# Extra 60-column products ahead of some TensorE steps, in a kernel with a planned order

## The chip, the cores and the metric

The kernel runs on one core of one Trainium2 chip. The metric is the device time of one execution in microseconds (us). A core has several engines that run side by side: TensorE (PE in the profile) multiplies matrices, ScalarE (ACT) and VectorE (DVE) compute elementwise and reduce, GpSimd (POOL) only sets up constants here, and SyncE (SP) issues DMA transfers. TensorE writes its products into PSUM, a memory of eight banks of 512 fp32 columns on 128 partitions; ScalarE and VectorE read them there.

## The reference

```python
scores = scale * np.matmul(q, k.transpose(0, 1, 3, 2))      # q, k, v: 4 x 8 x 576 x 64
scores = np.where(masks, scores, -1e9)                      # a window of 32; heads 4..7 dilated by 4
attn = softmax(scores)
x = np.matmul(attn, v)                                      # -> 2304 tokens x 512
h = x @ w_in                                                # 512 -> 1024
solu = h * softmax(h)
x = layernorm(solu) * g_ln @ w_out                          # 1024 -> 512
h = x @ w_in2                                               # 512 -> 2048
return softplus(h) @ w_out2                                 # 2048 -> 512
```

All inputs and the output are fp32. The kernel splits most operands into two fp16 halves, high and low, and adds three fp16 products (high-high, high-low, low-high).

## The kernel before, in words

The attention is cut into 28 pairs of blocks. A block takes 80 or 96 query rows of four heads. Its products are called QK (scores), PV (probabilities times values), and, for the first ten pairs, t, tp and tx (transposes by TensorE). The first ten pairs work in fp32; the others work in fp16 halves and transpose by DMA. Eighteen token tiles of 128 go through the first layer (m1a and m1b: 12 products of 512 columns each) and the normalisation. Nine groups of 256 tokens go through w_out (ya, yb: 24 products of 256 columns), the hidden layer (h: 24 products of 256 columns) and the output (o: 12 products of 512 columns). The weights are read as fp32, scaled and split; for the scale a small product sums squares over the partitions (w1im, w2o2m and the like, and pre0m to pre3m for q, k and v).

The order is written by a planner (class Plan, line 105). Every step is an operation with a cost per engine (`pe_cost`, line 203, for TensorE), the operations that it follows, and the buffers that it uses. A table of due times (DUE, line 254) gives priorities. The planner walks through time, starts on each engine the most urgent operation that is ready, and notes the start as `t0` (line 176). At the end (lines 1283 to 1285) each operation's function is called in that order. `pin` keeps each engine's instructions in the order in which they were called; the framework adds the semaphores by which one engine waits for another. So the planner fixes only each queue's order; at run time an instruction starts when its engine is free and its semaphores allow.

Four PSUM tiles, bank0 to bank3, of one bank each are shared among the small products:

```python
banks = [psum.tile([128, 512], FP32, name=f"bank{i}") for i in range(4)]      # line 398
ps_x.add(banks[1], place=taken[1])                                            # 402
for x in (1, 0, 2, 3):
    ps_v.add(banks[x], place=taken[x])                                        # 408
```

Bank 1 holds the output of PV in columns 0 to 259 and the transposed result of tx in columns 260 to 451 (`px` and `xt`, lines 871 and 872), and the sums for the scales in its first columns. VectorE or ScalarE reads PV's part to normalise it (into xf), and both read tx's part to cast it into xr, the input of the first layer. Columns 452 to 511 are written by nothing. `mm` (line 432) is one product. `eye`, a 128 x 128 identity in bf16, is made by GpSimd at the start, as is its fp32 twin `eye32`, which the first transposes need.

Of the kernel before, what the change touches and what calls it, by code (L numbers as in the profile page):

```python
# [216 lines left out]
def kernel(  # L217
# [12 lines left out]
    nc = tc.nc  # L230
# [57 lines left out]
    def mem(shape, dt, name):  # L288
        return const.tile(shape, dt, name=name)
# [3 lines left out]
    eye = mem([128, 128], BF16, "eye")  # L293
# [104 lines left out]
    banks = [psum.tile([128, 512], FP32, name=f"bank{i}") for i in range(4)]  # L398
# [13 lines left out]
    pin = tc.keep_in_program_order  # L412
# [19 lines left out]
    def mm(out, l, r, start, stop):  # L432
        pin(nc.tensor.matmul(out, l, r, start=start, stop=stop))  # L433
# [845 lines left out]
    for p in (qk_pool, qT_pool, kT_pool, pT_pool, xd_pool):  # L1279
        for s in p.slots:  # L1280
            if s[3] is not last_w and not s[3]:
                s[3].extend(last32)
    order = P.order()
    for o in order:
        o.fn(o.on)


# [28 lines left out]
```

## Time and profile before

| | |
|---|---|
| median of 3 runs | 772.14 us (771.76 to 773.48) |
| the profiled execution | 773.81 us, span 772.1 us |
| mean granted TensorE clock | 0.956 of full speed |
| busy: TensorE, VectorE, ScalarE | 92%, 75%, 62% |

The span runs from the first instruction to the last. A timeline row gives the start, the length of the run of like instructions, the engine, the source line (often that of a helper), the operation, output<-input, the shape and the count; in brackets stand the idle time of the engine before it and what ended that. [...] All views give times in us from the span's start.

### The profile page before, as it was taken

How to read it: one execution, taken by the hardware profiler on the slowest of the kernel's cores; microseconds unless marked ns; L12 is line 12 of the kernel's file. 1: busy time of each engine (PE TensorE's matmuls, PEld its weight loads, DVE VectorE, ACT ScalarE, POOL GpSimd, SP SyncE). 2: the span in 40 equal slices, each digit the busy share in tenths (PEclk: the TensorE clock that was granted, in tenths of full speed). 3: DMA queues.
4: the chain of work that ended last, by engine and by line, in shares of the span. 5: the costliest groups of instructions: out<-in, count | busy, mean ns of one | idle time of the engine just before them, and what ended most of it. 6: DMA issues, size and time to landing. Idle time of an engine off the chain costs nothing.

```text
span 772.1 us, 14234 instructions
## 1 busy us (share of the span) xinstructions
PE 708.1 (92%) x5176; PEld 495.2 (64%) x5176; DVE 579.9 (75%) x1646; ACT 478.0 (62%) x1057; POOL 3.5 (0%) x22
## 2 busy tenths in 40 slices
PE   6787989969968889999899999999999999999997
PEld 5574676745856447766756558676676568676673
DVE  1898978989999996696999997799955633534363
ACT  4575776757899856865787776656825524423351
POOL 1000000000000000000000000000000000000000
PEclk9999558968979999999999999999999999999999
DMA  8983773647895466824988788157403002100000
GB/s 223 253 259 132 207 178 104 175 104 164 157 183 138 93 160 176 220 60 107 176 163 145 149 145 160 36 110 123 83 11 82 1 1 56 28 1 28 1 28 28
DMA packets 187798, 89.80 MB, mean 116 GB/s; under 512 B 158032, under 2 KB 175440, under 8 KB 187728
## 3 DMA queue, kind: packets, MB, share of 16 engines
q1 hardware_dynamic: 187728, 88.90, 50.6%
q8 instruction: 40, 0.66, 0.4%
q14 instruction: 30, 0.25, 0.1%
HBM read 54.53 MB, written 4.72 MB: 77 GB/s over the span
## 4 chain that ended last, share of the span: by engine, by line
PE 46%; DVE 28%; ACT 11%; DMA 9%; issue 5%; SPq 0%; DVEq 0%; ACTq 0%
PE bank L433 23%; PE ps_w L433 21%; ACT a L415 4%; DVE s L941 3%; DVE W L424 3%; PE bank L436 2%; DMA pT<-p 2%; DVE E L424 2%; DVE r L424 2%; DVE p L427 2%; DMA E<-in_moe_w_out_dram 1%; DVE g L427 1%; DVE e L424 1%; ACT E L415 1%; ACT hl L415 1%
## 5 line engine op out<-in xcount | busy, mean ns | idle before, releaser
L433 PEld LDWEIGHTS <-W 128*128 128x128 f16 x2592 | 253.2, 98 | 46.3 <-issue 9.4
L433 PE MATMUL bank<-y,W 128*128 128x256 f16 x1728 | 199.0, 274 | 5.8 <-ACT r L415 2.4
L433 PE MATMUL ps_w<-W,g 128*128 128x512 f16 x864 | 194.8, 379 | 3.7 <-DVE s2i L419 1.3
L433 PEld LDWEIGHTS <-g 128*128 128x128 f16 x864 | 83.2, 98 | 97.0 <-DVE g L427 2.6
L433 PE MATMUL ps_w<-W,xr 128*128 128x512 f16 x432 | 106.0, 402 | 2.9 <-ACT osb L415 1.4
L415 ACT ACTIVATE a<-bank,invC 128x512 f32<-128x512 f32 x72 | 49.0, 681 | 85.1 <-PE bank L433 82.6
L433 PE MATMUL bank<-lnT,W 128*128 128x256 f16 x864 | 97.4, 273 | 2.2 <-DVE y L424 1.7
L415 ACT ACTIVATE a<-a 128x512 f32<-128x512 f32 x144 | 90.1, 627 | 2.5
L421 DVE TENSOR_SCALAR r<-bank,KR 128x512 f32<-128x512 f32 x44 | 33.0, 749 | 62.3 <-ACT a L415 57.7
L433 PEld LDWEIGHTS <-xr 128*128 128x128 f16 x432 | 43.7, 104 | 55.0 <-issue 14.0
L424 DVE SCALAR_TENSOR_TENSOR r<-a,KR,r 128x512 f32<-128x512 f32 x72 | 53.7, 746 | 14.8 <-ACT a L415 13.2
L415 ACT ACTIVATE s<-s 96x128 f32<-96x128 f32 (+3 forms) x144 | 43.6, 375 | 24.6 <-DVE s L421 18.7
L415 ACT ACTIVATE E<-E 128x768 f32<-128x768 f32 (+3 forms) x58 | 42.0, 725 | 18.0 <-DVE E L424 6.7
L427 DVE TENSOR_TENSOR g<-r,g 128x512 f16<-128x512 f32 x72 | 49.4, 687 | 3.2 <-DVE g L448 0.5
L941 DVE CUSTOM_DVE_ANT_0 s<-bank,band,bsc 96x128 f32<-96x128 f32 (+3 forms) x144 | 39.0, 324 | 1.5 <-PE bank L433 1.0
L433 PE MATMUL bank<-kT,qT 128*96 128x128 f16 (+7 forms) x288 | 31.2, 260 | 1.0 <-DMA kT<-qk 0.6
L415 ACT ACTIVATE y<-bank 128x512 f16<-128x512 f32 x16 | 9.5, 593 | 35.5 <-PE bank L433 35.5
L433 PEld LDWEIGHTS <-pT 128*96 128x96 f16 (+3 forms) x432 | 22.9, 125 | 13.1 <-DMA pT<-p 8.9
L433 PE MATMUL bank<-v,pT 128*96 128x65 f16 (+3 forms) x432 | 24.0, 207 | 7.5 <-DMA pT<-p 3.7
L415 ACT ACTIVATE e<-ps_w,st,bsc 128x1024 f32<-128x1024 f32 x16 | 19.2, 1200 | 18.3 <-DVE rs L419 9.5
L424 DVE SCALAR_TENSOR_TENSOR E<-E 128x512 int32<-128x512 int32 x44 | 28.6, 682 | 0.1
L1067 DVE TENSOR_REDUCE st<-ps_w 128x1 f32<-128x1024 f32 x18 | 21.8, 1218 | 8.8 <-PE ps_w L433 8.7
(196 smaller groups left out, 922.8 us busy)
## 6 DMA issues: line engine op xcount, KB each, us to landing
E<-in_moe_w_in_dram SPq DMA_DIRECT2D x18, 512.0 KB, 4.5
E<-in_moe_w_out_dram SPq DMA_DIRECT2D x18, 512.0 KB, 5.0
out_dram<-osb SPq DMA_DIRECT2D x18, 256.0 KB, 2.4
E<-in_q_dram SPq DMA_DIRECT2D x9, 384.0 KB, 3.3
E<-in_k_dram SPq DMA_DIRECT2D x9, 384.0 KB, 3.7
E<-in_v_dram SPq DMA_DIRECT2D x9, 384.0 KB, 3.5
W<-in_moe_w_in_dram SPq DMA_DIRECT2D x6, 512.0 KB, 6.5
W<-in_moe_w_out_dram SPq DMA_DIRECT2D x6, 512.0 KB, 5.2
```

What stands on the lines that cost most here:

```text
L415: pin(nc.scalar.activation(out=out, in_=in_, func=func, **kw))
L421: pin(nc.vector.tensor_scalar(out=out, in0=in0, scalar1=s1, scalar2=s2, op0=op0, op1=op1))
L424: pin(nc.vector.scalar_tensor_tensor(out=out, in0=in0, scalar=s, in1=in1, op0=op0, op1=op1, **kw))
L427: pin(nc.vector.tensor_tensor(out=out, in0=a, in1=b, op=op))
L433: pin(nc.tensor.matmul(out, l, r, start=start, stop=stop))
L436: pin(nc.tensor.transpose(out, in_, eye32[:in_.shape[0], :in_.shape[0]]))
L941: pin(nc.vector.tensor_tensor_reduce(out=sv()[:rows, h, :nk], in0=sb.t[:rows, h, :nk], in1=band[:rows, 48 - m:48 - m + nk], scale=sc[:rows ...
L1067: ({"DVE": (1.142, 0.14)}, lambda e: pin(nc.vector.tensor_reduce(out=col(0), in_=ph(), axis=AXX, op=ALU.max, negate=True)), [mb], [ps]),
```

## The change

Ahead of the loop that calls the operations, one product writes 60 columns that no other step uses. Then, for each TensorE operation that the planner starts before 300 us of its own time, the loop looks at the time between the end of the TensorE operation ahead of it and its start, both by the planner. It takes 0.3 us off, divides by 0.03 us, and issues that many products of the identity with its own first 60 columns into the same 60 columns of bank 1, just ahead of the operation. Nothing reads them. The planner, its costs and its order are as before.

```diff
     order = P.order()
+    spare = banks[1][:, 452:512]
+    mm(spare, eye, eye[:, 0:60], True, True)
+    free = 0.0
     for o in order:
+        if o.on == "PE":
+            if o.t0 < 300.0:
+                for _ in range(int((o.t0 - free - 0.3) / 0.03)):
+                    pin(nc.tensor.matmul(spare, eye, eye[:, 0:60], start=False, stop=False, skip_group_check=True))
+            free = o.t0 + o.opts["PE"][0]
         o.fn(o.on)
```

## Rows read from the trace of the kernel before

**Rows 1.** The page: busy time (share, instructions) of each engine; a DMA queue.
```profile
PE 708.1 (92%) x5176; PEld 495.2 (64%) x5176; DVE 579.9 (75%) x1646; ACT 478.0 (62%) x1057; POOL 3.5 (0%) x22
...
q8 instruction: 40, 0.66, 0.4%
```

**Rows 2.** By stretch: length, PE, PEld, DVE, ACT, POOL busy, granted clock, DMA, GB/s.
```profile
80.00:97.00 17.00, 17.00 (x69) 11.18 (x69) 16.23 (x45) 13.63 (x49) 0.00 (x0) 0.51 0.71 203
101.00:121.00 20.00, 19.16 (x100) 14.16 (x100) 16.66 (x54) 14.95 (x40) 0.00 (x0) 0.50 0.77 196
162.00:179.00 17.00, 13.29 (x64) 9.67 (x65) 15.02 (x70) 12.14 (x27) 0.00 (x0) 0.50 0.48 94
...
300.00:772.00 472.00, 454.56 (x3536) 316.05 (x3533) 323.38 (x906) 261.21 (x519) 0.00 (x0) 1.00 0.41 83
```

**Rows 3.** Timeline of TensorE: like work at either level.
```profile
52.30 2.02 PE L433 MATMUL bank<-qk,qT 64*96 64x128 f32 x8
...
153.25 1.11 PE L433 MATMUL bank<-kT,qT 64*96 64x128 f32 x8
...
116.71 4.93 PE L433 MATMUL ps_w<-W,xr 128*128 128x512 f16 x12
...
121.62 2.75 PE L433 MATMUL ps_w<-W,xr 128*128 128x512 f16 x12
```

**Rows 4.** Timeline of TensorE, the first 62 us.
```profile
4.20 0.79 PE L436 MATMUL bank<-eye,rk 80*128 80x80 f32 x4 [4.20 <-POOL eye L487]
...
7.25 1.48 PE L436 MATMUL bank<-eye,W 80*128 80x80 f32 x8 [1.72 <-DMA W<-in_k_dram]
...
23.43 1.25 PE L433 MATMUL bank<-xd,pT 80*80 80x65 f32 x8
...
28.36 0.58 PE L433 MATMUL bank<-band,eye 96*96 96x512 bf16 x1 [0.89 <-ACT qk L415]
...
32.53 1.33 PE L433 MATMUL bank<-xd,pT 80*80 80x65 f32 x8 [1.18 <-DVE xr L427]
...
40.30 1.33 PE L433 MATMUL bank<-qk,pT 80*80 80x65 f32 x8 [1.45 <-DVE xr L427]
...
62.01 1.01 PE L436 MATMUL bank<-eye,W 112*128 112x112 f32 x4 [3.88 <-ACT pT L415]
```

**Rows 5.** Timeline of VectorE, two reads of bank 1.
```profile
29.03 0.42 DVE L427 TENSOR_TENSOR xf<-bank,rs 80x256 f32<-80x256 f32 x1
...
32.01 0.47 DVE L427 TENSOR_TENSOR xr<-bank,xr 128x144 f16<-128x144 f32 x1
```

**Rows 6.** TensorE's timeline, and its weight loads by form (busy, mean ns).
```profile
187.88 2.78 PE L433 MATMUL bank<-y,W 128*128 128x256 f16 x24
190.50 0.61 PE L433 MATMUL bank<-kT,qT 128*96 128x128 f16 x8
...
241.06 0.62 PE L433 MATMUL bank<-v,pT 112*80 112x65 f16 x12
241.52 2.79 PE L433 MATMUL bank<-y,W 128*128 128x256 f16 x24
...
L433 PEld LDWEIGHTS <-W 128*128 128x128 f16 x2592 | 253.2, 98 | 46.3 <-issue 9.4
...
L433 PEld LDWEIGHTS <-pT 128*96 128x96 f16 x168 | 9.3, 125 | 8.1 <-DMA pT<-p 6.8 <-issue 0.2
```

**Rows 7.** Timeline of GpSimd at the start.
```profile
3.61 0.54 POOL L487 TENSOR_SCALAR_AFFINE_SELECT eye<-eye 128x128 bf16<-128x128 bf16 x2
```

**Rows 8.** Timelines of TensorE, VectorE and ScalarE at two later places.
```profile
162.42 1.33 PE L433 MATMUL bank<-qk,pT 80*80 80x65 f32 x8 [2.79 <-DVE st L419]
...
225.34 0.59 PE L433 MATMUL bank<-amw,ones 128*128 128x4 f32 x2 [6.79 <-ACT xf L415]
...
161.90 0.47 DVE L427 TENSOR_TENSOR xr<-bank,xr 128x96 f16<-128x96 f32 x2
...
224.39 0.90 ACT L415 ACTIVATE xf<-bank,rs 80x64 f32<-80x64 f32 x4
```

## The prediction

> **What bounds the kernel now.** I read the page's busy shares first, then busy time by stretch, then TensorE's timeline over the first 285 us, and last the readers of PSUM bank 1 on VectorE and ScalarE.
>
> TensorE is busy 708 of 772 us [rows 1]. From 300 us to the end it computes 454.56 of 472 us at the upper clock level, so whatever delay it carries at 300 us reaches the end nearly whole: only 17 us of idle stand behind it [rows 2]. The first 285 us are different. [...] The records of the clock begin only at 66.5 us, but the same eight fp32 products took 2.02 us at 52.30 and 1.11 at 153.25 [rows 3], so the first 62 us run at half too: some 62 + 17 + 20 + 17 us in all. Where a dense block begins cold it pays: twelve products of 512 columns took 4.93 us at 116.71 and 2.75 at 121.62 [rows 3].
>
> Next, what TensorE waits for. At 32.53 it stood 1.18 us behind VectorE's write to xr [rows 4]; that instruction reads bank 1 and ended at 32.01 + 0.47 = 32.48 [rows 5]. The product that waited writes columns 0 to 259 of bank 1 and uses none of xr's data; VectorE read columns 260 to 451. The last read of the columns that it overwrites ended at 29.03 + 0.42 = 29.45 [rows 5]. So these waits go by bank, not by column. The unused columns 452 to 511 are in that same bank.
>
> **The change, part by part.** Nothing is removed and no order moves. Added are products of the identity with its own first 60 columns, ahead of 27 of TensorE's steps. The number at each comes from the planner in the kernel's own text, run as it stands; I use its times for places and counts alone, never as durations. With the one ahead of the loop: 91 (before the first transposes, tk0), 13, 68, 9, 14, 29, 11, 43, 9, 1, 8, 143 (before tk5, the first 62 us); 10, 16, 7 (97 to 103 us); 47, 9, 5, 1, 51, 12 (159 to 175); 169, 3, 37 (before w2o2m and after it, 225 to 233); 15, 22, 41 (245 to 277). That is 884.
>
> *One added product.* The trace has none, so bounds. [...] I take 27.5 and 50 ns and keep 58 and 107 for the range.
>
> *When they may run.* Each burst writes bank 1, so it stands in TensorE's queue until every earlier reader of bank 1 on the other engines is done; a product of the real work behind it stands too. And TensorE's idle time is often just the wait for such a reader. The idle time ends, then the burst runs, then the work. Sums by stretch, lower level unless said:
>
> 1. Start. The identity is written until 3.61 + 0.54 = 4.15 us [rows 7], so 91 x 0.050 = 4.55 us run from there, to 8.7; tk0 stood at 4.20 [rows 4]: 4.5 later. The wait of 1.72 for a load at 7.25 takes back that much: +2.8.
> 2. To 45 us. The 68 stand before 23.43, where TensorE was not idle: +3.4. The 9 and 14 wait for the read that ends at 29.45, then 0.7: 30.2 in place of 28.36, +1.8. The 29 before 32.53 and the 43 before 40.30 follow a read of bank 1 that had itself ended the idle time (1.18 and 1.45 us) [rows 4, 5]: +1.45 and +2.15. The 13 and 9 are two more of this pattern: +0.65 and +0.45. The 11, 8 and 1 fit into idle time. +9.9.
> 3. tk5. Bank 1 is free, and 3.88 us of idle stand before 62.01 [rows 4]: 143 x 0.050 = 7.15, so +3.3; if half of them run at the upper level, 5.5, so +1.7. The block of four dozen dense products that follows then finds the clock up, worth about the 1.9 to 2.2 us that a cold dozen loses [rows 3]. 0, bounds -0.5 and +1.4.
> 4. 97 to 103 us: three small bursts behind readers, +1.0.
> 5. 159 to 175 us. The 47 follow VectorE's read that ends at 161.90 + 0.47 = 162.37; the work started at 162.42 [rows 8]: +2.35. The 9, 5, 51 and 12 are the same pattern with part of the wait left to fill: 0.2, 0.7, 1.15, 0.6. +5.0.
> 6. w2o2m. TensorE idles 6.79 us before 225.34, the longest wait of all [rows 8], and 169 products are put there. But ScalarE's reads of bank 1 end at 224.39 + 0.90 = 225.29 [rows 8]: none of them fits. All at the lower level 8.45 us, all at the upper 4.65; I take the middle, +6.6. VectorE's reduction of w2o2m stands in its own queue behind this, so it loses the time as well.
> 7. 245 to 277 us. The 15 wait for a read of ScalarE: +1.2. The 22 and 41 fit into idle time. +1.2.
>
> Sum 2.8 + 9.9 + 0 + 1.0 + 5.0 + 6.6 + 1.2 = 26.5 us. Of the 17 us of idle after 300 I let 2 absorb, since most of them follow chains that start on TensorE. So +24.5: from the profiled execution's 773.81 us, 772.1 of span and 1.7 around it, to 798.3. The median shown is 1.7 lower: 772.14 + 24.5 = 796.6, 797 us.
>
> Hidden costs that I put at nothing: the added instructions, 1,768 with their weight loads, are an eighth of what the core runs now; the page's queue for instructions moved 40 packets in 0.4% of 16 engines' span, 1.2 us each [rows 1], so five more are 6 us, beside TensorE's work as now, and 6 on top of the sum if a burst outruns them. The VectorE reads behind a burst wait for its end, but they read what a step ahead of it wrote, and the place behind is already counted.
>
> [...] Where the level is low, TensorE is mostly busy [rows 2], with fp32 products [rows 3]; dense 16-bit work raises it. [...]
>
> **Rivals.**
> - *The bursts hold the upper level* from the first one on, and the fp32 work between them with it. Then cold dense blocks gain about 2.2 us at each of five places, 10 in all; the 17.00 + 19.16 us of 80 to 121 us, less 10 of dense blocks, give 0.45 of 26, 12, by 1.11 against 2.02 [rows 2, 3]; the first 62 us, by the same share, up to 28 more. That is 50; half of it on TensorE's path, since it also waits there, gives 25, and the bursts, at 27.5 in place of 50 ns, some 15. It decides once more is gained than the bursts cost. Price: about -10, 762 us. For it: bursts are dense 16-bit work. Against it: no burst stands between 64 and 97 us, where the level is low while TensorE is busy all the time [rows 2]. Chance 0.09.
> - *Waits by columns, not by bank.* The bursts start when TensorE falls idle. Left are the start (2.8), the 68 (3.4), an overrun of up to 1.7 at the 169, and some tenths elsewhere, less what m1's dense block gains: about +5, 777 us. Against it: the wait at 32.53. Chance 0.09.
> - [...] Chance 0.08.
>
> **Numbers.** My forecast has 0.74, with 785 to 811 as its own range (tk5, w2o2m and the absorbed idle time at their bounds, and steps behind a late one that catch up). The range for all cases is 775 to 815: it takes in the second rival and leaves out the first, the third and the forecast's own tails, 0.2 together. A difference under 0.2% (1.5 us) can't be told from none. Of each of the first two rivals 0.01 falls within it: faster 0.08, same 0.02, slower 0.74 + 0.08 + 0.08 = 0.90.
>
> **What would show it.** Right: a burst of 91 from about 4.1 to 8.7 us; later bursts that begin just after a read of bank 1, above all the 169 only after ScalarE's four reads; 50 and 27.5 ns from one start to the next; a delay that is constant after 285 us; the level still low in most of the fp32 stretches. Wrong: bursts inside the idle time while another engine reads bank 1; a clock that stays up between 64 and 121 us; a gap of 40 us or more between TensorE's old and new start of the dense part, which would be the price of one product.

## The result, and the profile after

The changed kernel takes 781.28 us (median of 4 runs, 780.49 to 784.6) against 771.95 for the kernel before (4 runs, 770.9 to 773.48): ratio 1.0137, 95% interval 1.0112 to 1.0161. It is slower, as forecast, but by 9.3 us where 24.5 were forecast. It lies inside the range for all cases (775 to 815 us) and below the forecast's own (785 to 811): the prediction was wrong by the size. Its profiled execution took 780.7 us with a span of 779.0 and a mean granted clock of 0.947.

The page of after, busy time, as in [rows 1]:

```profile
PE 722.9 (93%) x6060; PEld 515.7 (66%) x6060; DVE 579.5 (74%) x1646; ACT 476.0 (61%) x1057; POOL 3.5 (0%) x22
```

There are 884 more products, and TensorE's busy time grew by only 14.8 us (708.1 to 722.9), though each of them took 27 to 50 ns. Something else on TensorE became shorter. By stretch, as in [rows 2], with four stretches of the first 62 us added, for which the trace of after has records of the clock:

```profile
8.20:14.90 6.70, 5.75 (x64) 4.49 (x62) 1.96 (x6) 5.55 (x18) 0.00 (x0) 1.00 0.65 142
15.00:28.50 13.50, 12.72 (x128) 10.73 (x127) 7.81 (x21) 5.82 (x20) 0.00 (x0) 0.50 0.90 259
28.70:35.30 6.60, 4.17 (x72) 3.49 (x72) 4.48 (x12) 3.68 (x11) 0.00 (x0) 1.00 0.94 309
49.20:62.00 12.80, 12.37 (x68) 10.19 (x68) 11.55 (x37) 10.13 (x33) 0.00 (x0) 0.50 0.87 254
80.00:97.00 17.00, 13.51 (x82) 10.07 (x81) 16.67 (x47) 13.21 (x44) 0.00 (x0) 0.69 0.67 196
101.00:121.00 20.00, 16.75 (x143) 13.31 (x142) 16.90 (x53) 15.30 (x38) 0.00 (x0) 0.74 0.66 157
162.00:179.00 17.00, 12.83 (x176) 11.30 (x175) 14.23 (x63) 10.37 (x29) 0.00 (x0) 0.80 0.35 80
```

Two things are to be seen. The level rises for a while in or behind the bursts of 91, 68, 43 and 143 products (at 8.1, 28.6, 45.7 and 66.1 us) and falls again under fp32 work (1.00, 0.50, 1.00, 0.50 down the first four rows). And in the three stretches in which before had 0.51, 0.50 and 0.50, after has 0.69, 0.74 and 0.80. These are the same times, not the same work, since after is 3.3 to 4.0 us late there; the same work (76.5 to 93.5, 97.6 to 117.6 and 158 to 175 us of before) had 0.61, 0.58 and 0.62, so part of the rise is the shift. From the mean clocks: after lost (1 - 0.947) x 779.0 / 0.5 = 83 us to the lower level, and the 8 us ahead of its first record with it: about 91. Before lost (1 - 0.956) x 772.1 / 0.5 = 68, and with the 66.5 us ahead of its first record, which count as 1.00, about 134. So some 40 us of the lower level are gone.

TensorE's timeline of after:

```profile
4.00 4.49 PE L1291 MATMUL bank<-eye 128*128 128x60 bf16 x90
8.33 0.48 PE L436 MATMUL bank<-eye,rk 80*128 80x80 f32 x4
...
10.57 0.80 PE L433 MATMUL bank<-kT,qT 64*80 64x80 f32 x8
...
14.59 0.82 PE L436 MATMUL bank<-eye,rk 128*128 128x128 f32 x4
...
31.42 1.11 PE L433 MATMUL bank<-kT,qT 64*96 64x128 f32 x8
...
34.17 0.96 PE L1291 MATMUL bank<-eye 128*128 128x60 bf16 x29 [1.35 <-DVE xr L427]
...
56.33 2.02 PE L433 MATMUL bank<-qk,qT 64*96 64x128 f32 x8
...
67.78 0.58 PE L436 MATMUL bank<-eye,W 112*128 112x112 f32 x4
68.20 10.53 PE L433 MATMUL ps_w<-W,xr 128*128 128x512 f16 x48
78.56 0.44 PE L436 MATMUL bank<-eye,W 80*128 80x80 f32 x4
...
166.42 1.45 PE L1291 MATMUL bank<-eye 128*128 128x60 bf16 x47 [2.79 <-DVE st L419]
167.71 0.77 PE L433 MATMUL bank<-qk,pT 80*80 80x65 f32 x8
...
228.75 6.88 PE L1291 MATMUL bank<-eye 128*128 128x60 bf16 x169 [6.21 <-ACT xf L415]
235.47 0.36 PE L433 MATMUL bank<-amw,ones 128*128 128x4 f32 x2
...
283.84 5.34 PE L433 MATMUL ps_w<-W,g 128*128 128x512 f16 x24
```

TensorE's timeline of before, the same steps:

```profile
8.92 1.35 PE L433 MATMUL bank<-kT,qT 64*80 64x80 f32 x8
...
14.88 1.12 PE L436 MATMUL bank<-eye,rk 128*128 128x128 f32 x4
...
28.87 2.02 PE L433 MATMUL bank<-kT,qT 64*96 64x128 f32 x8
...
62.81 12.37 PE L433 MATMUL ps_w<-W,xr 128*128 128x512 f16 x48
75.01 0.44 PE L436 MATMUL bank<-eye,W 80*128 80x80 f32 x4
...
217.94 0.61 PE L433 MATMUL bank<-v,pT 112*80 112x65 f16 x12
...
226.99 4.43 PE L433 MATMUL bank<-y,W 128*128 128x256 f16 x24
...
277.08 5.34 PE L433 MATMUL ps_w<-W,g 128*128 128x512 f16 x24
```

VectorE's timeline of after, the read of bank 1 ahead of the burst of 29:

```profile
33.65 0.47 DVE L427 TENSOR_TENSOR xr<-bank,xr 128x144 f16<-128x144 f32 x1
```

ScalarE's timeline of after, the four reads of bank 1 ahead of the 169:

```profile
227.81 0.89 ACT L415 ACTIVATE xf<-bank,rs 80x64 f32<-80x64 f32 x4
```

The bursts wait as predicted: 33.65 + 0.47 = 34.12 and the 29 start at 34.17; 227.81 + 0.89 = 228.70 and the 169 start at 228.75. Ninety products in 4.49 us are 50 ns each, 47 from 166.42 to 167.71 are 27 ns each. What the prediction has nowhere in its sum stands in between: eight products with kT took 0.80 us at 10.57 and 1.35 in before (8.92), and at 31.42 they took 1.11 where before's row of the same step (28.87) took 2.02.

How late TensorE is against before, step for step (start after less start before; the forecast is its own terms added up):

| step, start before | measured | forecast |
|---|---|---|
| first transposes, 4.20 [rows 4] | +4.1 | +4.5 |
| 128-column transposes, 14.88 | -0.3 | +2.8 |
| PV, 23.43 [rows 4] | +3.7 | +6.9 |
| QK, 52.30 [rows 3] | +4.0 | +12.7 |
| tk5, 62.01 [rows 4] | +5.8 | +16.0 |
| behind the block of 48, 75.01 | +3.5 | +12.7 |
| ahead of the 169, 217.94 | +4.0 | +18.7 |
| w2o2m, 225.34 [rows 8] | +10.1 | +25.3 |
| hidden layer, 277.08 | +6.8 | +26.5 |
| end of the span | +6.9 | +24.5 |

### The profile page after: what moved, and what is told of

Read it like the earlier page. It is cut to its first block, busy times and chain, and to the rows that moved or that the text cites. A ratio compares the mean times of both kernels' runs of the same rounds, so it can differ in the third digit from the quotient of the medians.

```text
span 779.0 us, 16002 instructions
## 1 busy us (share of the span) xinstructions
PE 722.9 (93%) x6060; PEld 515.7 (66%) x6060; DVE 579.5 (74%) x1646; ACT 476.0 (61%) x1057; POOL 3.5 (0%) x22
## 4 chain that ended last, share of the span: by engine, by line
PE 44%; DVE 27%; ACT 13%; DMA 9%; issue 5%; SPq 1%; POOL 0%; DVEq 0%; ACTq 0%; POOLq 0%
PE bank L433 19%; PE ps_w L433 19%; ACT a L415 4%; PE bank L1291 4%; DVE s L941 3%; DMA pT<-p 3%; DVE W L424 3%; PE bank L436 2%; DVE r L424 2%; ACT E L415 2%; DVE hl L427 2%; DVE E L424 1%; ACT hl L415 1%; ACT s L415 1%; DVE p L427 1%
## 5 line engine op out<-in xcount | busy, mean ns | idle before, releaser
L433 PE MATMUL ps_w<-W,xr 128*128 128x512 f16 x432 | 101.7, 390 | 3.1 <-DVE osb L424 1.4
L1291 PE MATMUL bank<-eye 128*128 128x60 bf16 x883 | 39.0, 213 | 20.9 <-ACT xf L415 8.9
L1291 PEld LDWEIGHTS <-eye 128*128 128x128 bf16 x883 | 38.8, 114 | 23.5 <-issue 19.7
L941 DVE CUSTOM_DVE_ANT_0 s<-bank,band,bsc 96x128 f32<-96x128 f32 (+3 forms) x144 | 38.9, 322 | 1.2 <-PE bank L433 0.6
L433 PE MATMUL bank<-kT,qT 128*96 128x128 f16 (+7 forms) x288 | 29.1, 250 | 0.5 <-DVE s L941 0.5
L424 DVE SCALAR_TENSOR_TENSOR E<-E 128x512 int32<-128x512 int32 x44 | 28.6, 682 | 0.1
```

The source lines that it names most:

```text
L424: pin(nc.vector.scalar_tensor_tensor(out=out, in0=in0, scalar=s, in1=in1, op0=op0, op1=op1, **kw))
L941: pin(nc.vector.tensor_tensor_reduce(out=sv()[:rows, h, :nk], in0=sb.t[:rows, h, :nk], in1=band[:rows, 48 - m:48 - m + nk], scale=sc[:rows ...
L1291: pin(nc.tensor.matmul(spare, eye, eye[:, 0:60], start=False, stop=False, skip_group_check=True))
```

## The experiments

All are the changed kernel with the edit shown; of the longer edits only the lines that matter are shown, with `...` where others are left out. Theory C: the bursts cost what the sum says, but long ones lift the clock for the fp32 work behind them, and that gives back some 17 to 19 us. Its rival S: the bursts cost less than the sum, because steps behind a late one had slack. Three more questions: what the waits on bank 1 cost, how much belongs to w2o2m, and which bursts pay.

### Bursts of fp32 products

The same places and, as nearly as I could set it, the same burst times, but of fp32 products. Every fp32 stretch of [rows 2] runs at the lower level (0.50 to 0.51), so these should not lift it. First with a quarter of the count:

```diff
-    mm(spare, eye, eye[:, 0:60], True, True)
+    mm(spare, eye32, eye32[:, 0:60], True, True)
...
-                for _ in range(int((o.t0 - free - 0.3) / 0.03)):
-                    pin(nc.tensor.matmul(spare, eye, eye[:, 0:60], start=False, stop=False, skip_group_check=True))
+                n = max(0, int((o.t0 - free - 0.3) / 0.03))
+                for _ in range(max(1, round(n / 4)) if n else 0):
+                    pin(nc.tensor.matmul(spare, eye32, eye32[:, 0:60], start=False, stop=False, skip_group_check=True))
```

> Each burst keeps its place, its bank and about its length, but is made of a quarter as many fp32 products of the fp32 identity (at least one), the kind of work beside which the clock was at its lower level in the kernel before. Theory C (the bursts of 16-bit products raised the clock, and what followed ran faster; that is what my sum left out): the give-back is gone, so 788 to 798 us, 16 to 25 over the kernel before, with the first rise of the clock only at m1's first dense block and about as many microseconds at the lower level as before (some 130). Theory S (the clock did little; late steps of TensorE ran into waits that were there anyway): 779 to 784 us, as with the 16-bit bursts.

Measured: 840.97 us (before 772.14), ratio 1.0869, interval 1.0806 to 1.0933. A miss, and one that decides nothing between C and S: an fp32 product shows as two records of some 215 ns (44 in 9.59 us for the first burst), 430 ns in all at the lower level, twice what the edit assumed. The bursts took 89.0 us instead of 35.4, each counted from its start to that of the work behind it, less TensorE's idle time. So an eighth:

```diff
-                for _ in range(max(1, round(n / 4)) if n else 0):
+                for _ in range(max(1, round(n / 8.3)) if n else 0):
```

> The fp32 bursts again, one product in place of 8.3, since in the run before one fp32 product of 60 columns took 430 ns at the lower level and 217 at the upper, about eight of the 16-bit ones; so each burst now lasts about as long as in the changed kernel (33.6 us in all there). Theory C (16-bit bursts give time back by raising the clock): no rise of the clock before m1's first dense block, TensorE 10 to 13 us late at tk5 in place of 4.0, and 790 to 803 us. Theory S (the late steps run into waits, whatever the clock does): 4 us late at tk5, 779 to 784 us.

Measured: 799.93 us (before 771.89), 1.0358, 1.0321 to 1.0395. Its bursts took 44.2 us, against 35.4 in after (the 33.6 of the expectation leaves out the last product of each burst). TensorE's timeline of this kernel:

```profile
4.68 4.90 PE L1294 MATMUL bank<-eye 128*128 128x60 f32 x22
9.37 0.75 PE L436 MATMUL bank<-eye,rk 80*128 80x80 f32 x4
...
18.28 1.12 PE L436 MATMUL bank<-eye,rk 128*128 128x128 f32 x4
...
63.18 2.02 PE L433 MATMUL bank<-qk,qT 64*96 64x128 f32 x8
...
68.80 7.40 PE L1294 MATMUL bank<-eye 128*128 128x60 f32 x34
...
235.90 0.61 PE L433 MATMUL bank<-v,pT 112*80 112x65 f16 x12
243.64 8.79 PE L1294 MATMUL bank<-eye 128*128 128x60 f32 x40 [7.13 <-ACT xf L415]
252.22 0.54 PE L433 MATMUL bank<-amw,ones 128*128 128x4 f32 x2
```

The transposes behind the first burst took 0.75 us here and 0.48 in after, the QK at 63.18 took 2.02 as before, and the first rise of the clock came at 78.2 us, in the dense block (1.00 from there to 95.2 us). The lateness at the steps of the table is now 18.28 - 14.88 = +3.4, 63.18 - 52.30 = +10.9, 235.90 - 217.94 = +18.0 and 252.22 - 225.34 = +26.9, and +26.1 at the end, where the forecast had 2.8, 12.7, 18.7, 25.3 and 24.5. Up to 217.94 its bursts took 31.1 us, near the forecast's own price for the 597 products up to there (597 x 0.050 = 29.9). With bursts that don't lift the clock the forecast's sum comes out within 2 us at each of these steps. S falls: slack did not take the time. C is shown. Its size is less than the 17 us (by the ratios) to 19 us (by the medians) between this kernel and after, since the bursts take 8.8 us more here. The work shows it directly: up to the step at 217.94 TensorE was occupied by real work (from row to row, without bursts and idle time) for 186.6 us in before, 181.3 here and 168.8 in after.

### Half the early products

```diff
-                for _ in range(int((o.t0 - free - 0.3) / 0.03)):
+                n = max(0, int((o.t0 - free - 0.3) / 0.03))
+                for _ in range(n // 2 if o.t0 < 50.0 else n):
```

> Half as many products in each of the bursts before 50 us of planned time (45, 6, 34, 4, 7, 14, 5, 21, 4 and 4), the others as in the changed kernel. Theory C: the bursts are too short to lift the clock, so half the products save nothing: TensorE is 4 to 6 us late at tk5 (4.0 in the changed kernel), with the level low from the start until the burst at tk5, and 780 to 783 us. If the cost goes with the number of products: 2 us late at tk5, 778 to 780 us.

Measured: 778.75 us (before 771.89), 1.0078, 1.0049 to 1.0106. TensorE's timeline:

```profile
3.99 2.43 PE L1294 MATMUL bank<-eye 128*128 128x60 bf16 x45
6.25 0.78 PE L436 MATMUL bank<-eye,rk 80*128 80x80 f32 x4
...
30.79 2.02 PE L433 MATMUL bank<-kT,qT 64*96 64x128 f32 x8
```

The burst of 45 did not lift the clock (0.78 us for the transposes, 2.02 for kT), nor did any burst before the 143, which begin at 61.50. The bursts up to the QK of 52.30 took 7.5 us and TensorE is 3.6 late there; with the full count they took 13.8 us and it is 4.0 late. Twice the bursts cost 0.4 us more, since the second half pays for itself in clock. So the trace goes with theory C (4.2 late at tk5, 4 to 6 expected), but the time doesn't: it lies in the range of the other expectation, that the cost goes with the number of products. It is 2.5 us below after's by the medians and 4.6 by the ratios. The end of this profiled execution, the longest of its runs, is 7.1 late against 6.9. Behind the block of 48 it is 2.0 late (77.02) where after is 3.5; where the gain of the faster runs lies stays open.

### The waits alone, and w2o2m

One product at each place leaves every wait on bank 1 and takes the bursts away; the other kernel leaves out the 169 alone:

```diff
-                for _ in range(int((o.t0 - free - 0.3) / 0.03)):
+                n = max(0, int((o.t0 - free - 0.3) / 0.03))
+                for _ in range(min(n, 1)):
```

> One product at each of the 27 places in place of a burst: the waits for bank 1 stay, the time of the bursts goes. If the time is in the bursts, as both theories say: 771 to 773.5 us, no change from the kernel before. Rival (the added waits for readers of bank 1 cost the time, whatever stands behind them): 777 us or more.

```diff
-                for _ in range(int((o.t0 - free - 0.3) / 0.03)):
+                n = max(0, int((o.t0 - free - 0.3) / 0.03))
+                for _ in range(n if o.name != "w2o2m" else 0):
```

> All bursts but the 169 ahead of w2o2m. In the trace TensorE fell behind by 6 us there and kept it to the end. If that delay is on the path: 775 us, 5 to 7 under the changed kernel (774 to 777). Rival (it would have been lost at the next waits anyway): 779 to 782 us.

Measured: 773.12 us with one product (before 772.14), 1.0004, 0.9977 to 1.0031: the waits alone cost nothing that can be measured. Without the 169: 775.6, 1.0038, 1.0007 to 1.0069, 5.7 us below after by the medians and (1.0137 - 1.0038) x 772 = 7.6 by the ratios; the forecast had 6.6 for that step and the trace of after has 10.1 - 4.0 = 6.1.

Then each burst into a PSUM bank whose tile has no user at that point of the order, where there is one (a helper, `idle_bank`, looks for it), and into bank 1 otherwise:

```diff
...
+                i = idle_bank(q) if n else None
+                to = spare if i is None else banks[i][:, 452:512]
-                    pin(nc.tensor.matmul(spare, eye, eye[:, 0:60], start=False, stop=False, skip_group_check=True))
+                    pin(nc.tensor.matmul(to, eye, eye[:, 0:60], start=x == 0 and i is not None, stop=False, skip_group_check=True))
```

> The same number of products at the same places, but each burst writes columns 452 to 511 of a bank that holds nothing at that point of the order, the one that fell free first; where none is free, bank 1 as before. By the planner this gives the 169 bank 0, whose last reader ends 6 us of planned time ahead of w2o2m, and moves 51, 12, 3, 37 and 22 and 41 too; before 62 us nothing moves ahead, since TensorE idles there because the banks are taken. If waits go by bank: the 169 run inside the idle time and the clock stays up, so 772 to 776 us, w2o2m within 1 us of its time in the kernel before plus the delay it had ahead (about 3). If the bank doesn't matter: 780 to 782 us, the burst of 169 behind ScalarE's four reads as now.

Measured: 778.79 us (before 772.14), 1.0076, 1.0043 to 1.0109. The place that it was about, on TensorE's timeline:

```profile
222.94 0.61 PE L433 MATMUL bank<-v,pT 112*80 112x65 f16 x12
223.38 4.81 PE L1317 MATMUL bank<-eye 128*128 128x60 bf16 x169
229.89 0.39 PE L433 MATMUL bank<-amw,ones 128*128 128x4 f32 x2 [1.69 <-ACT xf L415]
...
231.06 4.45 PE L433 MATMUL bank<-y,W 128*128 128x256 f16 x24
```

The 169 ran in the idle time, and w2o2m lost nothing there: it is 4.55 late, the step ahead of it 5.0. So the 6.1 us of after are the burst's own time, which the wait on bank 1 kept out of the idle time. The time is 3 us above what I expected all the same. The clock did not stay up: behind 1.69 us without work the 24 products took 4.45 us, as in before (4.43), where after's took 2.79 (at 236.63). And this kernel is 7.7 late at tk5, more than after: up to the QK of 52.30 its bursts and its work together take what after's take (45.3 and 45.2 us), and TensorE waits 2.3 us longer. Why it waits longer the runs do not show.

### Which bursts pay

The 91 at the start alone:

```diff
+                for _ in range(n if o.name == "tk0" else 0):
```

> Only the 91 products ahead of the first transposes. Theory C: 4 us late at the start, all of it given back by 15 us in a stretch at the upper level, so TensorE is within 0.7 us of the kernel before from tk2 on and the time is 770.5 to 773.5 us. Theory S: 2.3 to 2.8 us late after the wait for the load at 7.25, 774 to 775 us.

Measured: 769.28 us (before 771.89), 0.9957, 0.9936 to 0.9978: faster than before, and than I expected. Windows of this kernel, columns as in [rows 2]:

```profile
8.40:11.70 3.30, 2.85 (x33) 2.13 (x30) 0.10 (x1) 2.49 (x7) 0.00 (x0) 1.00 0.54 124
11.80:66.00 54.20, 42.84 (x211) 33.29 (x212) 42.98 (x117) 35.72 (x106) 0.00 (x0) 0.50 0.78 228
```

Behind the one burst the upper level lasts 3.3 us here, and the clock then stays down to 66 us. In after the same burst was followed by 6.7 us of it, from the same start; the two executions differ in that, and I don't know why. TensorE is 4.2 late at the first transposes, some 1.0 from 13 us on and 0.1 early at 217.94; where the 2.6 us that the median gains come from, the trace up to there does not show.

The next kernels aim at places where an empty bank and idle time meet; the first of them keeps the bursts from 159 to 175 us as they were. Early products work on an fp16 tile that VectorE fills at the start, so they need not wait for the identity:

```diff
+    warm = hl_pool.slots[0][0][:, 0, 0:128]
+    nc.vector.memset(warm, 0.5)
...
-    mm(spare, eye, eye[:, 0:60], True, True)
+    for x in range(100):
+        pin(nc.tensor.matmul(spare, warm, warm[:, 0:60], start=x == 0, stop=False, skip_group_check=True))
```

First with tk5, w2o2m raised to 240, and the later places but five:

```diff
+    less = {"w2o2m": 240}
...
-            if o.t0 < 300.0:
+            if 50.0 < o.t0 < 300.0 and not 80.0 < o.t0 < 100.0 and o.name not in ("h0.4", "PV11.1"):
...
+                n = less.get(o.name, n)
```

> A version made from what the runs showed. A burst of 100 at the start on an fp16 tile that VectorE fills, ready some 3 us before the identity, so that it ends at about 6 us, ahead of the load that the second pair of transposes waits for; no other burst before 45 us nor at 97 to 103 us nor the 15 and the 3; the 143 at tk5 and those from 159 to 175 us as they are; before w2o2m 240 products in bank 0, which is free there; 51, 12, 37, 22 and 41 in a free bank too. Theory C with waits by bank: 2 us won at the start, 0.5 each at tk5 and at 160 to 180, about 2 at w2o2m by a clock that stays up: 766 to 770 us. If early gains on TensorE are lost again in waits for VectorE (S in the other direction): 771 to 773 us.

Then with five places beside the early 100:

```diff
+    less = {"w2o2m": 240}
...
-            if o.t0 < 300.0:
+            if o.name in ("tk5", "w2o2m", "PV12.0", "o1.2", "PV13.1"):
...
+                n = less.get(o.name, n)
```

> Bursts only where TensorE's idle time holds them and the bank is free: 100 at the start on VectorE's fp16 tile, 143 at tk5, 240 before w2o2m, 37, 22 and 41 later, all but the first two in a bank that holds nothing there. Left out against the version before it: the bursts from 159 to 175 us, beside which TensorE went from 2.4 us early to 0.6 early. Theory C with waits by bank: 766.5 to 769.5 us. If early gains are lost in later waits: 770 to 772 us.

Measured: 770.85 (before 771.89), 0.9969, 0.995 to 0.9988; and 771.13 (before 772.35), 0.997, 0.9947 to 0.9993. Both gain less than expected. So the parts one by one. The 240 before w2o2m alone, without the early ones:

```diff
+    less = {"w2o2m": 240}
...
-            if o.t0 < 300.0:
+            if o.name == "w2o2m":
...
+                n = less.get(o.name, n)
```

> Only the burst ahead of w2o2m, 240 products in bank 0, which no engine reads there, so that they fill TensorE's idle time from 218 to 225 us. Theory C: the clock doesn't fall, so the dense block behind it takes 2.6 in place of 4.4 us and w2o2m stays within 0.5 us of its place: 769.5 to 771.5 us. If the gain is lost in the next wait, which is for a DMA: 771.5 to 773 us.

Measured: 772.06 (before 772.35), 0.9986, 0.9967 to 1.0006: nothing that can be told from none. TensorE's timeline:

```profile
225.38 2.79 PE L433 MATMUL bank<-y,W 128*128 128x256 f16 x24
229.56 0.65 PE L433 MATMUL bank<-v,pT 112*80 112x65 f16 x12 [1.39 <-DMA pT<-p]
```

The clock stayed up through the idle time: the 24 products behind it took 2.79 us in place of 4.43. The next step waits 1.39 us for a DMA, as it waited 1.36 in before, but this wait did not take the gain: the step starts 232.78 - 229.56 = 3.2 early, and 1.55 of that were there ahead of the burst (216.39 for 217.94). So in this execution, one of the fastest of its twelve, some 1.7 us are won at this place, and the median doesn't show them; where they are lost stays open.

The 143 at tk5 alone, in a bank that is free:

```diff
-            if o.t0 < 300.0:
+            if o.name == "tk5":
```

> Only the 143 ahead of tk5, in bank 1, which is free there, as in the changed kernel. tk5 1 to 2 us later, the dense block behind it 2 us shorter: 770.5 to 773 us, TensorE 0 to 0.7 us early from the second dozen of that block on. If filling idle time were a gain by itself: 769 us or less; if its delay stayed: 773.5 or more.

Measured: 767.53 us (before 772.35), 0.9926, 0.9901 to 0.9951: the fastest of all, 4.8 us under before by the medians and 5.7 by the ratio, where after is at 1.0137. TensorE's timeline:

```profile
56.29 5.79 PE L1318 MATMUL bank<-eye 128*128 128x60 bf16 x143
61.92 0.58 PE L436 MATMUL bank<-eye,W 112*128 112x112 f32 x4
62.34 10.53 PE L433 MATMUL ps_w<-W,xr 128*128 128x512 f16 x48
72.70 0.44 PE L436 MATMUL bank<-eye,W 80*128 80x80 f32 x4
```

The burst fills the idle time and overruns it (TensorE is 1.63 early ahead of it, 0.09 at tk5 behind it), the level is up when the block of 48 starts, and that takes 10.53 us in place of 12.37. Net at the step behind: 75.01 - 72.70 = 2.3 early, of which 1.6 were there before the burst (50.67 for 52.30). So the trace places 0.7 us of the gain; where the rest of the median's comes from, it does not show. The time also lies where I expected it if filling idle time were a gain by itself (769 us or less), and that rival is not excluded: no run with a burst at this place alone leaves the level down.

The 100 early products alone (no place in the loop), then with the 143 at tk5, then tk5 alone with half its products:

```diff
+    less = {"tk5": 71}
...
+            if o.name == "tk5":
...
+                n = less.get(o.name, n)
```

> Only the 100 products at the start, on the fp16 tile that VectorE fills by about 1 us, so that they end at 6 us, before the load that the second transposes wait for. Theory C: the upper level for one or two stretches of the fp32 work behind them, TensorE 1.4 to 3 us early to the middle of the kernel: 769 to 771 us. If early gains are lost in later waits: 771.5 to 773 us. If the burst of 91 on the identity gained something by itself at the end, this one, ahead of it by 3 us, gains at least as much.

> The 100 products at the start, on VectorE's tile, and the 143 at tk5, and no others. Each alone came out ahead of the kernel before, by 0.5% and 0.7%. If both gains are the clock's and lie in different stretches, they add as far as TensorE sets the time: 764 to 767.5 us. If the second only repeats what the first gains (both end in the same wait later): 767.5 to 769.5 us.

> Half the burst at tk5, 71 products, which end inside the idle time of 3.9 us, so that tk5 is not late. Theory C (what counts is that the clock rises before the dense block): if 71 products are long enough to lift it, tk5 in place and the block 2 us shorter, 767 to 769.5 us; if not, nothing changes, 771 to 773 us, and the block begins at the lower level as in the kernel before. If filling the idle time were a gain by itself, whatever the level: 768 us or less with the block as slow as before.

Measured: early alone 769.21 (before 772.35), 0.9951, 0.993 to 0.9972; both 769.24 (before 771.81), 0.9961, 0.9941 to 0.9982; 71 at tk5 770.1, 0.9979, 0.9958 to 1.0. The early ones, on TensorE's timeline:

```profile
1.12 4.89 PE L1288 MATMUL bank<-hl 128*128 128x60 f16 x100 [1.12 <-DVE hl L474]
5.85 0.47 PE L436 MATMUL bank<-eye,rk 80*128 80x80 f32 x4
...
12.12 0.94 PE L436 MATMUL bank<-eye,rk 128*128 128x128 f32 x4
```

A burst that ends at 5.9 and not 8.4 us lets the same transposes start 1.65 late instead of 4.13, and with the clock up TensorE is 14.88 - 12.12 = 2.8 early at the 128-column transposes. Not all of that is the burst's: the kernels with tk5 alone and with w2o2m alone, which do the same work as before up to their burst, are 1.63 early at the QK of 52.30 (50.67) and 1.55 at 217.94 (216.39). Taken off, that leaves some 1.2 for the burst, as an estimate. The two gains don't add: 764 to 767.5 us were expected if they did. The 71 came out above what I expected (767 to 769.5 us). They also lifted the level ahead of the block (10.53 us), and TensorE is 3.7 early behind it (71.27 for 75.01), 1.55 of it from the start; but then it waits 1.93 us for ScalarE, and at the step of 76.50 (74.75) only 0.2 us of the gain remain.

## Why the prediction was wrong

*What held.* The unit price: 50 and 27 ns were the measured spacings (90 products in 4.49 us, 47 in 1.29), so the third rival, with 58 and 107 ns a product, is out. No run shows the 27.5 ns of the forecast, nor the 58 and 107 ns of its range; in their place the runs showed 27 ns at the upper level and, as the forecast took it, 50 at the lower. Waits by bank: both fences of the readers show it, with 50 ns between the end of the reads and the first product, and moving the 169 to another bank removed the whole loss at w2o2m (4.55 late there, 5.0 at the step ahead); the second rival (waits by columns) is out. Point 6, w2o2m: +6.6 forecast, +6.1 in the trace, 5.7 to 7.6 from the kernel without it. Point 3, tk5: 0 forecast with -0.5 as a bound, and +4.0 to +3.5 is -0.5.

*What failed.* Points 1, 2, 4 and 5 of the sum: they charged each burst in full and left the work between the bursts at the lower level. I knew the ratio (2.02 against 1.11 us, [rows 3]) and used it for the first rival alone, as if the level were either held for good or, but for the dense block behind tk5, never gained. It was gained for a while: point 1 came out at -0.3 for +2.8, point 2 at 4.0 + 0.3 = +4.3 for +9.9, points 4 and 5 together at 4.0 - 3.5 = +0.5 for +6.0. These are 14 of the 17.6 us by which the end of the span in the trace lies under the forecast (24.5 - 6.9).

Up to 52 us the bursts took 13.8 us and TensorE is 4.0 late. Of the 9.8 between, 2.3 are idle time that went, above all the wait for the load at 7.25, which the forecast had. The other 7.5 are shorter work, 31.4 us in place of 38.9. The level was up for 6.8 + 6.8 + 3.4 = 17 us of it (8.1 to 14.9, 28.6 to 35.4 and 45.7 to 49.1 us); by the share 0.45 of [rows 3] that gives 7.7 us, as an estimate. In 159 to 175 us the 47 ran at the upper level, and so did what came next (eight products in 0.77 us in place of 1.33); and the block of 36 behind the last burst began with the level up, so that TensorE is 180.34 - 175.02 = 5.3 late at its start and 188.11 - 184.84 = 3.3 behind it. The eighth-count fp32 kernel, where this is missing, has the forecast's sums within 2 us at five steps: the main cause is this term.

*What else was off.* The 2 us that idle time behind 300 us was to absorb were not absorbed: the hidden layer starts 6.8 late and the end is 6.9 late. That the time lies inside the range for all cases is luck: its lower end, 775, was set for the second rival, which is out.

*Why I saw it wrong.* Against the first rival stood that TensorE is busy all of 80 to 97 us at half the clock, with no burst near. That is true, and the level did fall again each time under fp32 work (0.50 at 15 to 28.5 us, TensorE 94% busy). It says that a burst does not hold the level; it does not say that the level falls at once. So the rival came true in part, and one with a partial gain was missing. At 220 us, in TensorE's longest idle time, 240 products across the gap kept the clock up (the 24 behind them took 2.79 us), and 169 with 1.69 us of idle behind them did not (4.45 us).

*Point 7* was +1.2 and came out at 6.8 - 10.1 = -3.3. About 1 us of it is the block at 226.99, which took 4.43 us in before and 2.79 in after. Much of the rest may be the one execution of before, which is argued and not shown: in the kernel with single products the same hidden layer starts 274.41 - 277.08 = 2.7 earlier than before, and only 0.5 earlier at 249.37, but its span ends only 0.2 earlier. Before's profiled execution took 773.81 us, 1.9 above its median, and after's 0.6 below its own, so the traces differ by 6.9 us where the medians differ by 9.3.

TensorE's timeline of the kernel with single products:

```profile
274.41 5.34 PE L433 MATMUL ps_w<-W,g 128*128 128x512 f16 x24
```

## What to carry to other kernels

Work that changes the clock has two prices, its own time and the time of what runs behind it at the other level (here eight products with kT in 0.80 us or in 1.35); write both into the sum, and take a partial gain as a case of its own. Filler should go where it waits for nobody: into an empty PSUM bank, and into idle time directly ahead of dense work. In these runs that paid at tk5 and at the start, by less than 1%, and at w2o2m the gain could not be told from none. Spare columns in a bank that others read cost a wait for those readers: with the 169 in bank 1 w2o2m lost 6.1 us, with them in an empty bank nothing. A wait that ends on another engine's read of the same bank is not room for filler into that bank: here 6 us idle took none of 169 products.

## What the runs showed of the hardware

- A burst of 45 bf16 products (2.43 us) at the start left the clock down (0.78 us for the transposes behind it); 90 of them (4.49 us) lifted it (0.48); 11 fp32 products (22 records) of 4.90 us did not (0.75), and neither did 7.40 us of them at 68.8 (the step behind took 0.96 us, in after 0.58).
- An fp32 product of 60 columns and 128 rows takes 430 ns at the lower level (44 records in 9.59 us), the bf16 one 50: nearly nine times as much.
- The same start and the same burst of 91 were followed by 6.7 us of the upper level in one kernel (after) and 3.3 in another (the 91 alone), so a single trace of the clock's steps is not the kernel's habit.
- In the run of 240 products alone TensorE stopped 0.70 us after 172 of them, a wait that the view calls "issue". The 143 of after, of the half counts and of tk5 alone (5.99, 4.90 and 5.79 us) and the 169 of after and of the kernel with idle banks (6.88 and 4.81 us) had no such stop.
